# One VectorE instruction that scales, copies and reduces attention scores, and spare products for TensorE, in a fused attention and mixture-of-experts kernel

## The chip, the cores and the metric

The kernel runs on one core of a Trainium2 chip. A core has five engines, each with an in-order queue of its own: TensorE (PE in the profile; its weight loads are shown apart as PEld), VectorE (DVE), ScalarE (ACT), GpSimd (POOL) and SyncE (SP), whose queue issues nearly all DMAs of this kernel. The time of a run is the device time of one launch in microseconds (us); lower is better.

## The reference, cut to what matters

Two stages follow each other. The first is attention over 8 batches of 8 heads, 576 tokens of 64 numbers each, in which scores that lie more than `tau` below the row's maximum are dropped:

```python
scores = scale * np.matmul(q, k.transpose(0, 1, 3, 2))        # scale = 1/8
thresh = np.max(scores, axis=-1, keepdims=True) - tau
scores = np.where(scores >= thresh, scores, -1000000000.0)
scores = scores - np.max(scores, axis=-1, keepdims=True)
attn = np.exp(scores)
attn = attn / (np.sum(attn, axis=-1, keepdims=True) + 1e-09)
out = np.matmul(attn, v)
```

The second takes the 4608 rows of 512 numbers that this gives. Rows whose product with `w_skip` is positive go to one of 8 experts (the largest of 8 logits), each a two-layer network of 512 to 1024 to 512 with a ReLU between; the result is weighted by the gate and added to the row. The other rows are copied.

## The kernel before, in words

**Pairs, chunks, units.** The attention works on 32 pairs (8 batches, 4 pairs of heads each). A pair's q and k lie in one SBUF tile (`raw`), one head on partitions 0 to 63 and the other on 64 to 127. Its 576 query rows are cut into four chunks of 128 rows, in which each head is a unit of its own (`u`), and a last chunk (`M`) with the remaining 64 rows of both heads as a single unit. So a pair has nine units of 128 rows by 576 scores, and the kernel 288.

**What is done with a unit.** TensorE writes its scores in two rounds (`score`, line 519; `score_m`, line 529, for the chunk M) into PSUM. VectorE finds the negated maximum of each row (`top`, line 542, into a column of the tile `mx`). ScalarE computes exp(score - maximum) from PSUM into SBUF (`expo`, line 556). A small instruction (`thr`, line 549, VectorE or GpSimd) turns the maximum into the threshold. VectorE reads the scores from PSUM once more, compares them with the threshold and multiplies the exponential by the outcome (`mask`, line 564). The product is split into two half-precision parts, a rounded copy (`fph`, lines 329 and 331, ScalarE or VectorE) and the rest (`fpl`, line 618, mostly GpSimd). Two DMAs transpose the parts (line 623), and TensorE multiplies them with v (`av`, line 659, 30 products a chunk). The scale of 1/8 is put on q beforehand (`qs`, lines 357 and 359, once per pair).

**What a unit holds.** The eight banks of PSUM are shared out as six for scores (`sall`, three slots of two banks; a chunk takes two slots, the chunk M one), one for `gps` (transposes and logits) and one for the output of `av`. A score slot is given back by `mask`: `ring.free("sps", [k])` stands behind it. The exponentials have three buffers (`e`), the masked chunks two (`p`) and one (`pm`).

**What sets the order.** Every operation is put into a planner (`Plan`) with its engine or engines, a cost, the operations and buffers it depends on, and a key. `Plan.run` plays the program through with these costs: of the operations that are ready on an engine, the one with the smallest key comes next, and the order in which it starts them is the order in each engine's queue. The keys are the position in the sequence (nine per pair) plus an offset per kind of operation from the table `OFF`; a smaller one goes first. On the chip the queues keep this order and wait on semaphores. The planner also interleaves the preparation of v (`plan_v`), the logits of the experts and the bookkeeping of the routing.

**The second stage** begins when the attention's rows are in memory; its order is written out by hand behind `pl.run`, and the change leaves it alone.

Of the kernel before, what the change touches and what calls it, by code (L numbers as in the profile page):

```python
# [49 lines left out]
NBK = (NM + 1) * H + H // 2  # L50
NTL = NM * H
SPB = 3
GPB = 1
EB = 3
PFB = 2
HLB = 3
PTB = 3
TMB = 2
# [10 lines left out]
DISS = 0.65  # L69
DLAT = 0.9  # L70
OFF = dict(
    ld=-5.6, qs=49.8, S=-7.6, mx=-31.6, th=-71.4, e=-43.7, p=-83.3, ph=-25.7, pl=-26.3, tt=-8.5, av=4.9, cp=45.3, x=19.3, xw=3.1, row=126.2, rsp=-41.2, init=13.4, L1=-66.1, sc=-73.8, d0=50.9, phD=-64.0, v=8.8, vsp=4.8, V2=15.9,
)

class Op:
# [16 lines left out]

class Plan:
    def __init__(self):
        self.ops, self.rings = [], {}

    def take(self, name, bufs):
        return [(name, bufs)]
# [30 lines left out]
    def run(self, look):  # L129
# [14 lines left out]
        while left:  # L144
            best = None
            for e, c in cand.items():
                if not c:
                    continue
                if e == "PE":
                    c = [(max(free[e], x[0]) + (MODE[x[2].half] if x[2].half != half else 0.0), x[1], x[2]) for x in c]  # L150
                m = max(free[e], min(x[0] for x in c))
                x = min((x for x in c if x[0] <= m + look), key=lambda x: (x[1], x[0]))
                t = max(free[e], x[0])
                if best is None or t < best[0]:
                    best = (t, e, x[2])
            t, e, o = best
            o.t0, o.on = t, e
            if e == "PE":
                half = o.half
            o.t1 = free[e] = t + o.eng[e]  # L160
            for i, x in enumerate(o.xfer):
                link = max(link, t + (i + 1) * o.eng[e] / len(o.xfer) + DISS) + x
                o.t1 = link
            code = o.fn.__code__
            if code.co_argcount and code.co_varnames[0] == "e":
                o.fn(e)
            else:
# [12 lines left out]
def attn_moe_kernel(ctx: ExitStack, tc: tile.TileContext, qk, vl, vt, tau, wg, w1, w2, out):  # L180
# [17 lines left out]
    tpos = cp.tile([P, 1], F32, name="tpos")  # L198
    nc.vector.tensor_scalar(tpos, taub, 0.0, 0.125, op0=ALU.is_ge, op1=ALU.mult)
    wgt = cp.tile([P, NDT, 16], F32, name="wgt")  # L200
    onesr = cp.tile([1, P], F32, name="onesr")

    why = "a count of routed tokens bounds it"
    cnt = cp.tile([P, E], F32, name="cnt")
# [142 lines left out]
    def plan_pair(g):  # L347
        k = STEP * g

        def load():  # L350
            T["raw", g] = wtile(F32, "raw")[:, 0 : 2 * S]
            nc.sync.dma_start(T["raw", g], qk[g])

        def qs(e):
            q = T["raw", g][:, 0:S]
            if e == ACT:
                nc.scalar.activation(q, q, AF.Copy, scale=tpos)
            else:
                (nc.gpsimd if e == POOL else nc.vector).tensor_scalar(q, q, tpos, None, op0=ALU.mult)
# [133 lines left out]
    def plan_chunk(g, i):  # L493
# [44 lines left out]
        def top(u):  # L538
            if i == 0 and u == 0:
                T["mx", g] = ap_.tile([P, 2, STEP], F32, name="mx", tag="mx", bufs=3)  # L540
            c = 2 * i + u
            nc.vector.tensor_reduce(  # L542
                T["mx", g][:, 0, c : c + 1], bank(u), AX.XY, ALU.max, negate=True
            )

        def thr(e):
            cs = slice(2 * i, 2 * i + len(units))
            m = T["mx", g]
            (nc.gpsimd if e == POOL else nc.vector).tensor_scalar(
                m[:, 1, cs], m[:, 0, cs], -1.0, taue, op0=ALU.mult, op1=ALU.subtract  # L550
            )

        def expo(u):
            T["e", g, i, u] = e = ap_.tile([P, 2, HS], F32, name="e", tag="e", bufs=EB)
            c = 2 * i + u
            nc.scalar.activation(e, bank(u), AF.Exp, bias=T["mx", g][:, 0, c : c + 1])  # L556

        def mask(u):
            if M:
                T["p", g, i] = ap_.tile([P, 1, S], F32, name="pm", tag="pm", bufs=1)  # L560
# [12 lines left out]
        if M:  # L573
            ss = [pl.op(n + OFF["S"], score_m, [T["in", g]] + ring.take("sps", 3), {PE: 0.97}, half=True)]
        else:
            ss = []
            for r in range(2):
                ss.append(
                    pl.op(n + OFF["S"] + 0.1 * r, lambda r=r: score(r), [T["in", g]] + ring.take("sps", 3), {PE: 0.485}, half=True)
                )  # L580
        T.setdefault(("Sop", g), []).extend(ss)
        ms, es, ks = [], [], []
        for u in units:
            deps = ring.take("mx", 3) if i == 0 and u == 0 else [(T["m0", g],)]
            m = pl.op(n + OFF["mx"] + 0.1 * u, lambda u=u: top(u), ss + deps, {DVE: 0.67})
            if i == 0 and u == 0:
                T["m0", g] = m
            ms.append(m)
            es.append(pl.op(n + OFF["e"] + 0.1 * u, lambda u=u: expo(u), [m] + ring.take("e", EB), {ACT: 0.64}))
        t = pl.op(n + OFF["th"], thr, ms, {DVE: 0.12, POOL: 0.2})  # L590
        for u in units:
            take = [(ks[0],)] if u else ring.take("pm", 1) if M else ring.take("p", PFB)
            k = pl.op(n + OFF["p"] + 0.1 * u, lambda u=u: mask(u), [t, es[u]] + take, {DVE: 0.67})
# [163 lines left out]
    def plan_x(k, key, deps, src, last=False):  # L757
# [17 lines left out]
        t = pl.op(k, tr, deps + (ring.take("sps", SPB) if last else ring.take("gps", GPB)), {PE: 0.434})  # L775
# [999 lines left out]
```

## Time and profile before

| | |
|---|---|
| median of 3 runs | 1357.37 us (1357.23 to 1360.33) |
| profiled execution | 1357.51 us, of which the span from first to last instruction is 1355.7 us |
| busy in the span | TensorE 902.6 us, VectorE 815.8, GpSimd 579.2, ScalarE 465.6 |
| attention stage (0 to 1045 us of the span) | VectorE 665.3 us busy, TensorE 631.7, GpSimd 452.6, ScalarE 358.1 |
| second stage (1045 us to the end) | TensorE 270.8 of 311 us busy |

Busy time is the union of an engine's instructions. Matmuls are pipelined, so that a busy TensorE is not one at its peak. "PEclk" is the clock granted to TensorE as a share of full speed (2.4 GHz); it has two levels, 1.2 and 2.4 GHz, so that 0.67 is a mean over time. Each row of a group of instructions gives line, engine, operation, output and inputs by the program's names, shapes and count, then busy time and mean duration, then the engine's idle time just before these instructions and what ended it.

### The profile page before, as it was taken

The numbers are of one execution on the slowest core, as the hardware profiler recorded it, in microseconds if no ns is written. First come the engines' busy times: TensorE is split into PE (matmuls) and PEld (weight loads), VectorE is DVE, ScalarE is ACT, GpSimd is POOL, SyncE is SP. The second block draws the span as 40 slices with busy tenths as digits, with TensorE's granted clock in tenths as the row PEclk, the third lists the DMA queues.
The fourth block names the chain that finished last, engine by engine and source line by source line (L and its number), as shares of the span: only waits on it lengthen the run. The fifth ranks groups of instructions, "written<-read, shape, count | busy, mean of one in ns | idle before, by whom it ended". The sixth has DMA issues, their size and how long they took to land. (4 is left out here: it accounts for less than half of the span.)

```text
span 1355.7 us, 21156 instructions
## 1 busy us (share of the span) xinstructions
PE 902.6 (67%) x8210; PEld 696.9 (51%) x8210; DVE 815.8 (60%) x1422; ACT 465.6 (34%) x740; POOL 579.2 (43%) x394
## 2 busy tenths in 40 slices
PE   4555556656666565565565656766545688999996
PEld 3344334444445354344453544544425567989995
DVE  5667565676557667655666676557664234555872
ACT  2234322333334233323433333334233124435442
POOL 3443334343446435235553442446335205555552
PEclk7767766776667567577766665567667598999998
DMA  5655674676556765946584676565666226554540
GB/s 155 138 122 106 143 156 96 121 172 133 106 111 137 158 111 116 198 97 119 112 195 99 119 161 137 100 109 102 143 141 139 85 86 208 164 163 160 176 172 23
DMA packets 387781, 179.30 MB, mean 132 GB/s; under 512 B 354231, under 2 KB 354999, under 8 KB 387680
## 3 DMA queue, kind: packets, MB, share of 16 engines
q1 hardware_dynamic: 383056, 167.78, 56.0%
q0 software_dynamic: 4480, 10.15, 2.3%
q8 instruction: 65, 1.06, 0.3%
q14 instruction: 36, 0.29, 0.1%
q10 hardware_dynamic: 144, 0.00, 0.0%
HBM read 67.76 MB, written 24.65 MB: 68 GB/s over the span
## 5 line engine op out<-in xcount | busy, mean ns | idle before, releaser
L519 PE MATMUL sps<-raw 64*128 64x288 f32 x1024 | 267.7, 653 | 373.0 <-DVE p L564 306.0
L618 POOL TENSOR_TENSOR hla<-p,hla 128x1152 f16<-128x1152 f32 x119 | 282.5, 2374 | 392.4 <-ACT hla L329 206.4
L556 ACT ACTIVATE e<-sps,mx 128x576 f32<-128x576 f32 x288 | 199.7, 737 | 550.5 <-DVE mx L542 405.6
L519 PEld LDWEIGHTS sps<-raw 64*128 64x128 f32 x1024 | 129.9, 280 | 445.0 <-DVE p L564 230.7
L542 DVE TENSOR_REDUCE mx<-sps 128x1 f32<-128x576 f32 x288 | 206.1, 752 | 205.0 <-PE sps L519 103.8
L564 DVE SCALAR_TENSOR_TENSOR p<-sps,mx,e 128x576 f32<-128x576 f32 x256 | 197.7, 812 | 113.0 <-ACT e L556 102.8
L659 PEld LDWEIGHTS <-PTa 128*128 128x128 f16 x3840 | 181.8, 119 | 43.4 <-issue 35.9
L659 PE MATMUL avp<-Vh,PTa 128*128 128x65 f16 x2560 | 193.6, 225 | 3.3 <-DMA PTa<-hla 3.2
L659 PE MATMUL avp<-Vl,PTa 128*128 128x64 f16 x1280 | 184.1, 224 | 0.0
L1396 POOL TENSOR_TENSOR wl<-wr,wh 128x1024 fp32r<-128x1024 f32 x28 | 72.3, 2601 | 29.4 <-ACT wh L1395 24.1
L329 ACT ACTIVATE hla<-p 128x1152 f16<-128x1152 f32 x52 | 60.5, 1163 | 61.5 <-issue 49.4
L1433 PE MATMUL hps<-xh,wh 128*128 128x288 f32 (+4 forms) x224 | 69.1, 308 | 0.1
L1433 PE MATMUL hps<-xl,wh 128*128 128x288 f32 (+4 forms) x224 | 67.9, 303 | 0.0
L1433 PE MATMUL hps<-xh,wl 128*128 128x288 f32 (+4 forms) x224 | 67.8, 303 | 0.0
L709 POOL TENSOR_TENSOR xb<-a,z 128x512 f32<-128x512 f32 x32 | 39.0, 1218 | 55.3 <-DVE z L700 47.1
L1395 ACT ACTIVATE wh<-wr 128x1024 fp32r<-128x1024 f32 x60 | 60.6, 1050 | 0.0
L331 DVE CAST hla<-p 128x1152 f16<-128x1152 f32 x76 | 59.3, 780 | 1.0
L1495 PE MATMUL yps<-wh,QK 128*128 128x512 f32 (+2 forms) x224 | 57.5, 407 | 1.7 <-ACT wh L1395 1.5
L529 PE MATMUL sps<-raw 64*64 64x288 f32 (+2 forms) x320 | 58.1, 512 | 0.0
L1396 DVE TENSOR_TENSOR wl<-wr,wh 128x1024 fp32r<-128x1024 f32 x32 | 52.1, 1642 | 7.9 <-ACT wh L1395 7.4
L529 PEld LDWEIGHTS sps<-raw 64*64 64x64 f32 x320 | 33.1, 184 | 39.1 <-issue 29.7
L564 DVE SCALAR_TENSOR_TENSOR pm<-sps,mx,e 128x576 f32<-128x576 f32 x32 | 26.1, 817 | 43.2 <-PE sps L519 43.2
(241 smaller groups left out, 1429.6 us busy)
## 6 DMA issues: line engine op xcount, KB each, us to landing
wr<-in_w SPq DMA_DIRECT2D x31, 1024.0 KB
raw<-in_qk SPq DMA_DIRECT2D x32, 576.0 KB
vraw<-in_vl SPq DMA_DIRECT2D x32, 256.0 KB
out<-xb SPq DMA_DIRECT2D x32, 256.0 KB
xs<-xb SPq DMA_DIRECT2D x32, 256.0 KB
PTa<-hla SPq DMA_TRANSPOSE x256
vraw<-in_vt SPq DMA_DIRECT2D x8, 128.0 KB
TM<-hm SPq DMA_TRANSPOSE x64
```

What stands on the lines that cost most here:

```text
L329: nc.scalar.activation(dst, src, AF.Copy)
L331: nc.vector.tensor_copy(dst, src)
L519: nc.tensor.matmul(bank(h, j)[:, 0:HS], x[hs[h], i * P : i * P + P], x[hs[h], k0 : k0 + HS], start=True, stop=True)
L529: nc.tensor.matmul(bank(0, j)[hs[h], o : o + w], x[hs[h], NM * P : S], x[hs[h], S + c0 : S + c0 + w], start=True, stop=True, skip_group_ch ...
L542: nc.vector.tensor_reduce(T["mx", g][:, 0, c : c + 1], bank(u), AX.XY, ALU.max, negate=True)
L556: nc.scalar.activation(e, bank(u), AF.Exp, bias=T["mx", g][:, 0, c : c + 1])
L564: nc.vector.scalar_tensor_tensor(T["p", g, i][:, u].rearrange("p (a b) -> p a b", a=2), bank(u), T["mx", g][:, 1, c : c + 1], T.pop(("e", ...
L618: (nc.gpsimd if e == POOL else nc.vector).tensor_tensor(hl[:, lo0 : lo0 + w], T.pop(("p", g, i)).rearrange("p a b -> p (a b)"), hl[:, 0:w] ...
L659: nc.tensor.matmul(o[:, 0:e], x[:, w_, cs], y[:, vb, 0:e], start=first and j == 0, stop=kt == NM and j == 2, skip_group_check=True,)
L1395: nc.scalar.activation(w[0][:, sl], rs, AF.Copy)
L1396: lo[q % 2].tensor_tensor(w[1][:, sl], rs, w[0][:, sl].bitcast(F32), op=ALU.subtract)
L1433: nc.tensor.matmul(hp_[:, 0:cap], w_, x, start=(i == 0), stop=(i == len(mm) - 1))
```

## The change

`top` becomes one instruction that reads the scores from PSUM, multiplies them by -1/8, adds a tile of zeros (`none16`, bfloat16), writes the result to an SBUF tile `s` (four buffers) and writes its minimum to the column of `mx`. `expo` and `mask` read `s` in place of PSUM; `expo` writes into the chunk's tile `p`, and `mask` works on it in place, with `is_le` for `is_ge` since the sign is turned. The score slot is given back behind `top` (`ring.free("sps", [m])`). The scaling of q (`qs`) is gone, so that `score` depends on the load of `raw` alone. There are two score slots in place of three; of the two banks set free one goes to `gps` (two buffers) and one to `rest`, which nothing reads: where the plan leaves TensorE idle for more than 0.4 us, `fill` puts products of zeros (512 columns) into it, for six tenths of the rest of the gap at 0.22 us each. `p` has three buffers, `pm` two. The table `OFF` is replaced as a whole, and so the order of every queue of the attention stage.

```diff
-SPB = 3
-GPB = 1
-EB = 3
-PFB = 2
+GPB = 2
+SB = 4
+PFB = 3
+NSL = 2
+FILL = (0.4, 0.22, 0.6)
 OFF = dict(
-    ld=-5.6, qs=49.8, S=-7.6, mx=-31.6, th=-71.4, e=-43.7, p=-83.3, ph=-25.7, pl=-26.3, tt=-8.5, av=4.9, ...
+    ld=-63.5, qs=-113.0, S=-99.4, mx=-53.9, th=-2.3, e=-9.8, p=-0.5, ph=-18.0, pl=11.4, tt=-64.0, av=31.6, ...
 )
             if e == "PE":
+                if self.fill and free[e] > 0:
+                    gap = t - free[e] - FILL[0]
+                    for _ in range(int(gap * FILL[2] / FILL[1]) if gap > 0 else 0):
+                        self.fill(half)
                 half = o.half
...
-    sall = ps_s.tile([P, 6, 512], F32, name="sps")
-    slots = [(0, 1), (2, 3), (4, 5)]
+    sall = ps_s.tile([P, 2 * NSL, 512], F32, name="sps")
+    slots = [(2 * i, 2 * i + 1) for i in range(NSL)]
+    rest = ps_s.tile([P, 512], F32, name="rest")
...
-        qe = {POOL: 1.25, DVE: 0.42, ACT: 0.57} if g else {DVE: 0.42}
-        T["in", g] = pl.op(k - OFF["qs"], qs, [o], qe, off={DVE: OFF["d0"], ACT: OFF["d0"]} if g else {})
+        T["in", g] = o
...
-            nc.vector.tensor_reduce(
-                T["mx", g][:, 0, c : c + 1], bank(u), AX.XY, ALU.max, negate=True
+            T["s", g, i, u] = ap_.tile([P, S], F32, name="s", tag="s", bufs=SB)
+            nc.vector.tensor_tensor_reduce(
+                T["s", g, i, u].rearrange("p (a b) -> p a b", a=2),
+                bank(u),
+                none16[:, 0:S].rearrange("p (a b) -> p a b", a=2),
+                tneg8,
+                TOP,
+                ALU.add,
+                ALU.min,
+                T["mx", g][:, 0, c : c + 1],
             )
...
-            nc.scalar.activation(e, bank(u), AF.Exp, bias=T["mx", g][:, 0, c : c + 1])
+            nc.scalar.activation(
+                T["p", g, i][:, u], T["s", g, i, u], AF.Exp, bias=T["mx", g][:, 0, c : c + 1], scale=-1.0
+            )
...
             nc.vector.scalar_tensor_tensor(
-                T["p", g, i][:, u].rearrange("p (a b) -> p a b", a=2),
-                bank(u),
-                T["mx", g][:, 1, c : c + 1],
-                T.pop(("e", g, i, u)),
-                op0=ALU.is_ge,
-                op1=ALU.mult,
+                p, T.pop(("s", g, i, u)), T["mx", g][:, 1, c : c + 1], p, op0=ALU.is_le, op1=ALU.mult
             )
...
-            m = pl.op(n + OFF["mx"] + 0.1 * u, lambda u=u: top(u), ss + deps, {DVE: 0.67})
+            m = pl.op(n + OFF["mx"] + 0.1 * u, lambda u=u: top(u), ss + deps + ring.take("s", SB), {DVE: 0.67})
+            ring.free("sps", [m])
...
-            ring.free("sps", [k])
-            ring.free("e", [k])
+            ring.free("s", [k])
...
+    def fill(half):
+        r = D if half else P
+        nc.tensor.matmul(rest, none16[0:r, 0:P], none16[0:r, 0:512], start=True, stop=True, skip_group_check=True)
+    pl.fill = fill
```

## Rows read from the trace of the kernel before

**Rows 1.** Busy time of each engine in two stretches of the span, the attention stage and the rest: stretch, its length, then PE, PEld, DVE, ACT and POOL busy with the count of instructions, granted clock, mean busy share of the DMA engines, GB/s.

```profile
0.00:1045.00 1045.00, 631.74 (x6597) 454.80 (x6598) 665.29 (x1169) 358.08 (x558) 452.59 (x314) 0.67 0.64 129
1045.00:1356.00 311.00, 270.83 (x1618) 242.13 (x1616) 150.54 (x253) 107.51 (x182) 126.56 (x80) 0.92 0.42 141
```

**Rows 2.** Groups of instructions by line in the attention stage, shapes kept apart: busy us, mean ns of one, then the engine's idle us before them and what ended it.

```profile
L618 POOL TENSOR_TENSOR hla<-p,hla 128x1152 f16<-128x1152 f32 x119 | 282.5, 2374 | 392.4 <-ACT hla L329 206.4 <-issue 119.5 <-DVE hla L331 61.9
L542 DVE TENSOR_REDUCE mx<-sps 128x1 f32<-128x576 f32 x288 | 206.1, 752 | 205.0 <-PE sps L519 103.8 <-PE sps L529 72.6 <-ACT e L556 28.6
L556 ACT ACTIVATE e<-sps,mx 128x576 f32<-128x576 f32 x288 | 199.7, 737 | 550.5 <-DVE mx L542 405.6 <-DVE z L700 44.5 <-PE avp L659 35.8
L564 DVE SCALAR_TENSOR_TENSOR p<-sps,mx,e 128x576 f32<-128x576 f32 x256 | 197.7, 812 | 113.0 <-ACT e L556 102.8 <-POOL xb L709 5.8 <-issue 3.1
L564 DVE SCALAR_TENSOR_TENSOR pm<-sps,mx,e 128x576 f32<-128x576 f32 x32 | 26.1, 817 | 43.2 <-PE sps L519 43.2
```

**Rows 3.** Waits over the whole span: who waited for whom, us in total, times, longest us.

```profile
ACT e L556 <- DVE mx L542: 405.6, 120, 8.2
PE sps L519 <- DVE p L564: 306.0, 99, 6.3
...
DVE mx L542 <- PE sps L519: 103.8, 85, 2.8
DVE p L564 <- ACT e L556: 102.8, 111, 1.3
...
DVE mx L542 <- PE sps L529: 72.6, 32, 3.6
...
DVE pm L564 <- PE sps L519: 43.2, 29, 1.6
...
DVE mx L542 <- ACT e L556: 28.6, 32, 1.2
```

**Rows 4.** Instructions of all engines in order of time, from 502 to 519 us, neighbours of one kind merged: start us, us, engine, line, operation, tiles, count, and in brackets the engine's idle time before and who ended it.

```profile
502.07 1.24 PE L519 MATMUL sps<-raw 64*128 64x288 f32 x8 [1.04 <-DVE p L564]
...
503.24 1.69 PEld L659 LDWEIGHTS <-PTa 128*128 128x128 f16 x30
...
503.36 1.42 DVE L542 TENSOR_REDUCE mx<-sps 128x1 f32<-128x576 f32 x2 [0.55 <-PE sps L519]
...
504.90 1.37 ACT L556 ACTIVATE e<-sps,mx 128x576 f32<-128x576 f32 x2 [4.51 <-DVE mx L542]
...
506.36 1.54 DVE L564 SCALAR_TENSOR_TENSOR p<-sps,mx,e 128x576 f32<-128x576 f32 x2 [1.02 <-ACT e L556]
...
507.95 0.76 PE L519 MATMUL sps<-raw 64*128 64x288 f32 x4 [1.07 <-DVE vki L430]
...
509.76 1.88 PEld L659 LDWEIGHTS <-PTa 128*128 128x128 f16 x60
...
511.43 0.74 ACT L556 ACTIVATE e<-sps,mx 128x576 f32<-128x576 f32 x1 [3.84 <-DVE mx L542]
...
512.20 0.76 DVE L542 TENSOR_REDUCE mx<-sps 128x1 f32<-128x576 f32 x1 [0.89 <-ACT e L556]
...
518.38 2.29 PE L519 MATMUL sps<-raw 64*128 64x288 f32 x8 [0.91 <-DVE pm L564]
```

**Rows 5.** Single lines with the shortest, the median and the longest duration in ns: the masks of before, VectorE's subtraction of two SBUF tiles in two widths (the rows of line 618), a reduction of two numbers, and a ScalarE instruction of the same width that reads SBUF.

```profile
L564 DVE SCALAR_TENSOR_TENSOR p<-sps,mx,e x256: 799/816/820, 17.4 to 1033.3; 128x576 f32<-128x576 f32 x128
...
L618 DVE TENSOR_TENSOR hm<-pm,hm x13: 747/750/950, 47.6 to 811.3; 128x576 f16<-128x576 f32 x13
L618 DVE TENSOR_TENSOR hla<-p,hla x9: 1345/1351/1359, 114.0 to 1037.2; 128x1152 f16<-128x1152 f32 x9
...
L413 DVE TENSOR_REDUCE vmx<-vmx x8: 137/144/146, 15.8 to 822.1; 128x1 f32<-128x2 f32 x8
...
L357 ACT ACTIVATE raw<-raw,tpos x25: 758/772/783, 43.7 to 911.7; 128x576 f32<-128x576 f32 x25
```

**Rows 6.** The same view for VectorE instructions that read SBUF alone, and their groups' busy time and mean.

```profile
L549 DVE TENSOR_SCALAR mx<-mx,taue x138: 199/220/2400, 16.0 to 1031.2; 128x2 f32<-128x2 f32 x111, 128x1 f32<-128x1 f32 x27
...
L331 DVE CAST hm<-pm x25: 445/454/2020, 43.0 to 1003.2; 128x576 f16<-128x576 f32 x25
...
L549 DVE TENSOR_SCALAR mx<-mx,taue 128x2 f32<-128x2 f32 (+1 forms) x138 | 44.3, 339 | 0.6
L331 DVE CAST hm<-pm 128x576 f16<-128x576 f32 x25 | 24.9, 995 | 0.2
...
L1396 DVE TENSOR_TENSOR wl<-wr,wh x32: 1204/1224/7616, 1099.8 to 1329.4; 128x1024 fp32r<-128x1024 f32 x32
```

**Rows 7.** VectorE and GpSimd in order of time near 536 us: start us, us, engine, line, operation.

```profile
535.89 2.40 DVE L549 TENSOR_SCALAR mx<-mx,taue 128x2 f32<-128x2 f32 x1
...
535.91 2.36 POOL L618 TENSOR_TENSOR hla<-p,hla 128x1152 f16<-128x1152 f32 x1
```

**Rows 8.** A product of 512 columns in the second stage, and a stretch of that stage (columns as in the first group); then the load of q and k in SyncE's queue.

```profile
L1495 PE MATMUL yps<-wh,QK 128*128 128x512 f32 (+2 forms) x224 | 57.5, 407 | 1.7 <-ACT wh L1395 1.5 <-DVE QK L1465 0.2
...
1150.00:1200.00 50.00, 50.00 (x263) 44.25 (x261) 27.27 (x43) 20.13 (x31) 27.47 (x14) 1.00 0.56 185
...
SPq L352 <- PE sps L529: 49.2, 15, 7.4
```

More of the change, by code (lines that the diff above doesn't have):

```diff
@@ L52 @@
 SPB = 3
-GPB = 1
-EB = 3
-PFB = 2
+GPB = 2
+SB = 4
+PFB = 3
+NSL = 2
+TOP = 3.0e38
+FILL = (0.4, 0.22, 0.6)
 HLB = 3
@@ L71 @@
 OFF = dict(
-    ld=-5.6, qs=49.8, S=-7.6, mx=-31.6, th=-71.4, e=-43.7, p=-83.3, ph=-25.7, pl=-26.3, tt=-8.5, av=4.9, cp=45.3, x=19.3, xw=3.1, row=126.2, rsp=-41.2, init=13.4, L1=-66.1, sc=-73.8, d0=50.9, phD=-64.0, v=8.8, vsp=4.8, V2=15.9,
+    ld=-63.5, qs=-113.0, S=-99.4, mx=-53.9, th=-2.3, e=-9.8, p=-0.5, ph=-18.0, pl=11.4, tt=-64.0, av=31.6, cp=-20.0, x=28.2, xw=39.6, row=38.9, rsp=74.8, init=19.6, L1=-102.6, sc=-126.0, d0=16.6, phD=43.5, v=45.4, vsp=-12.1, V2=35.8,
 )
@@ L94, in __init__ @@
     def __init__(self):
-        self.ops, self.rings = [], {}
+        self.ops, self.rings, self.fill = [], {}, None
     def take(self, name, bufs):
@@ L197, in attn_moe_kernel @@
     nc.scalar.dma_start(taub, tau.rearrange("(a b) -> a b", b=1).broadcast_to([P, 1]))
-    tpos = cp.tile([P, 1], F32, name="tpos")
-    nc.vector.tensor_scalar(tpos, taub, 0.0, 0.125, op0=ALU.is_ge, op1=ALU.mult)
+    tneg8 = cp.tile([P, 1], F32, name="tneg8")
+    nc.vector.tensor_scalar(tneg8, taub, 0.0, -0.125, op0=ALU.is_ge, op1=ALU.mult)
     wgt = cp.tile([P, NDT, 16], F32, name="wgt")
     onesr = cp.tile([1, P], F32, name="onesr")
+    none16 = cp.tile([P, S], BF16, name="none16")
+    nc.vector.memset(none16, 0.0)
     why = "a count of routed tokens bounds it"
@@ L352, in load @@
             nc.sync.dma_start(T["raw", g], qk[g])
[L354 to L359, printed above, removed]
         o = pl.dma(k - OFF["ld"], load, ring.take("wr", WRB) + T["start"], [2.2], 0.46)
-        qe = {POOL: 1.25, DVE: 0.42, ACT: 0.57} if g else {DVE: 0.42}
-        T["in", g] = pl.op(k - OFF["qs"], qs, [o], qe, off={DVE: OFF["d0"], ACT: OFF["d0"]} if g else {})
+        T["in", g] = o
         if g == 0:
@@ L548, in thr @@
             m = T["mx", g]
-            (nc.gpsimd if e == POOL else nc.vector).tensor_scalar(
-                m[:, 1, cs], m[:, 0, cs], -1.0, taue, op0=ALU.mult, op1=ALU.subtract
-            )
+            (nc.gpsimd if e == POOL else nc.vector).tensor_scalar(m[:, 1, cs], m[:, 0, cs], taue, None, op0=ALU.add)
         def expo(u):
-            T["e", g, i, u] = e = ap_.tile([P, 2, HS], F32, name="e", tag="e", bufs=EB)
-            c = 2 * i + u
-            nc.scalar.activation(e, bank(u), AF.Exp, bias=T["mx", g][:, 0, c : c + 1])
-        def mask(u):
             if M:
-                T["p", g, i] = ap_.tile([P, 1, S], F32, name="pm", tag="pm", bufs=1)
+                T["p", g, i] = ap_.tile([P, 1, S], F32, name="pm", tag="pm", bufs=2)
             elif u == 0:
@@ L563, in mask @@
             c = 2 * i + u
-            nc.vector.scalar_tensor_tensor(
-                T["p", g, i][:, u].rearrange("p (a b) -> p a b", a=2),
-                bank(u),
-                T["mx", g][:, 1, c : c + 1],
-                T.pop(("e", g, i, u)),
-                op0=ALU.is_ge,
-                op1=ALU.mult,
+            nc.scalar.activation(
+                T["p", g, i][:, u], T["s", g, i, u], AF.Exp, bias=T["mx", g][:, 0, c : c + 1], scale=-1.0
+            )
+        def mask(u):
+            c = 2 * i + u
+            p = T["p", g, i][:, u]
+            nc.vector.scalar_tensor_tensor(
+                p, T.pop(("s", g, i, u)), T["mx", g][:, 1, c : c + 1], p, op0=ALU.is_le, op1=ALU.mult
             )
         if M:
-            ss = [pl.op(n + OFF["S"], score_m, [T["in", g]] + ring.take("sps", 3), {PE: 0.97}, half=True)]
+            ss = [pl.op(n + OFF["S"], score_m, [T["in", g]] + ring.take("sps", NSL), {PE: 0.97}, half=True)]
         else:
@@ L578, in plan_chunk @@
                 ss.append(
-                    pl.op(n + OFF["S"] + 0.1 * r, lambda r=r: score(r), [T["in", g]] + ring.take("sps", 3), {PE: 0.485}, half=True)
+                    pl.op(n + OFF["S"] + 0.1 * r, lambda r=r: score(r), [T["in", g]] + ring.take("sps", NSL), {PE: 0.485}, half=True)
                 )
@@ L588, in plan_chunk @@
             ms.append(m)
-            es.append(pl.op(n + OFF["e"] + 0.1 * u, lambda u=u: expo(u), [m] + ring.take("e", EB), {ACT: 0.64}))
+            take = [(es[0],)] if u else ring.take("pm", 2) if M else ring.take("p", PFB)
+            es.append(pl.op(n + OFF["e"] + 0.1 * u, lambda u=u: expo(u), [m] + take, {ACT: 0.64}))
         t = pl.op(n + OFF["th"], thr, ms, {DVE: 0.12, POOL: 0.2})
         for u in units:
-            take = [(ks[0],)] if u else ring.take("pm", 1) if M else ring.take("p", PFB)
-            k = pl.op(n + OFF["p"] + 0.1 * u, lambda u=u: mask(u), [t, es[u]] + take, {DVE: 0.67})
-            ring.free("sps", [k])
-            ring.free("e", [k])
+            k = pl.op(n + OFF["p"] + 0.1 * u, lambda u=u: mask(u), [t, es[u]], {DVE: 0.67})
+            ring.free("s", [k])
             ks.append(k)
@@ L773, in ev @@
             copy(e, xf, T.pop(("X", key)))
-        t = pl.op(k, tr, deps + (ring.take("sps", SPB) if last else ring.take("gps", GPB)), {PE: 0.434})
+        t = pl.op(k, tr, deps + (ring.take("sps", NSL) if last else ring.take("gps", GPB)), {PE: 0.434})
         x = pl.op(k + 0.3, ev, [t] + ring.take("xf", 2), {ACT: 0.478})
```

## The prediction, made before the changed kernel was run

> **What bounds the kernel now.** I begin with the busy times by stretch [rows 1]. In the second stage TensorE is busy for 271 of 311 us, and the change leaves that stage alone. In the attention stage no engine is full: VectorE, the busiest, has 665 of 1045 us and stands idle for 380; the granted clock of TensorE averages 0.67, between its levels of 1.2 and 2.4 GHz. So waits set the pace there. The groups by line tell where VectorE's idle time lies [rows 2]: 205.0 us before the reductions, 113.0 and 43.2 before the masks, 18.5 elsewhere. The list of waits names the partners [rows 3]: the reductions wait for scores (103.8 and 72.6 us), the masks for exponentials (102.8) and, in the chunk M, for TensorE (43.2), and TensorE's scores wait for masks (306.0). That is a ring, and the timeline shows it going round without overlap [rows 4]: scores 502.07 to 503.31, two reductions to 504.78, two exponentials to 506.27, two masks to 507.90, the next scores at 507.95. Each step begins about 0.1 us after the one before: 5.9 us a turn, of which VectorE works for 3. The third slot doesn't help, since a chunk needs two and gets the second only from a mask.
>
> **The change part by part.** All sums are made against the profiled execution (1357.5 us), 0.1 us above the median of the runs, so I take them as one.
>
> *The slot.* It now comes free behind the first VectorE step instead of behind the masks. Scores of the next chunk can then be made while VectorE masks, and by the keys (mx -53.9, p -0.5) the reduction goes ahead of a mask when both are ready. The exponential of one chunk lies beside VectorE's other work. Four buffers `s` allow two chunks in flight.
>
> *The new reduction* has no row. Nearest is the mask of before, which also reads PSUM and an SBUF tile and writes 128x576: 816 ns [rows 5]. Lower end: the reduction itself, 752 ns [rows 2]. Upper end: the mask plus a small reduction of 144 ns for reading out the minimum [rows 5], 960 ns. I take 816: 288 x (816 - 752) = +18 us (0 to +60).
>
> *The mask* now reads two SBUF tiles. Nearest: the subtraction of two SBUF tiles in the same width, 750 ns [rows 5], against 812 to 817: 288 x 63 ns = -18 us. The upper end is the wait below.
>
> *A new wait.* VectorE's instructions on SBUF alone are sometimes held up by GpSimd. A threshold, median 220 ns, took 2.40 us beside a GpSimd subtraction of 2.36 us and ended with it [rows 7]. The means stand above the medians: threshold 339 against 220, the cast of `pm` 995 against 454 [rows 6]. The masks of before, with one input in PSUM, never exceed 820 ns [rows 5]. The mask becomes an instruction that can be held. The two masks of a chunk run back to back, so there are 160 groups; ends 0 (as the masks of before) and 0.54 us (as the cast). Between 0.12 and 0.54 I take 0.3: 160 x 0.3 = +48 us (0 to +86). Behind a held mask stand the next reduction and so the slot, and TensorE waits for that.
> [...]
>
> VectorE's busy time becomes 665 + 18 - 18 + 48 = 713 us.
>
> *VectorE's idle time.* 18.5 us elsewhere stays. The masks' waits (102.8 and 43.2) all but go, since the exponential lies a chunk ahead and M's mask reads no PSUM: I leave 20. The single wait of a reduction for an exponential, 0.9 us once a pair and 28.6 us in all [rows 3, 4], shows that the column tile `mx` is guarded as a whole: a reduction follows the exponentials sent before it. Two exponentials (1.37 us) now lie beside two masks (1.4 us), so I leave the 28.6 as they are. The scores: 1.24 us a chunk at the high clock, 2.29 at the low one [rows 4], against about 2.1 us of other VectorE work (two masks, a threshold, at times a cast). At the high clock that covers them; at the low one, with 30 products of v in front (0.94 to 1.69 us [rows 4]) partly beside the reductions, about 0.5 us is missing. Today the scores cost 176.4 / 160 = 1.1 us a chunk; I take 0.6, which is 96 us (0 to 176). Sum: 18.5 + 20 + 28.6 + 96 = 163 us in place of 380.
>
> Attention 713 + 163 = 876 us against 1045: -169. Forecast 1357.5 - 169 = 1188, rounded to **1190 us**.
>
> *Edits at nothing.* Without `qs` ScalarE loses 25 instructions of 0.77 us [rows 5], beside its 687 us of idle time. The exponential reads SBUF: 0.77 in place of 0.74 us, on an engine that stays below half. More buffers of `p`, `pm` and `gps` can only take waits away. The loads of q and k (one DMA a pair) move behind the transposes, row stores and loads of v in SyncE's queue (key +63.5 in place of +5.6); four buffers and two pairs of lead hide that. If not, scores wait at each pair's start; the load's longest wait now is 7.4 us [rows 8], and 2 us a pair would be 64 us.
>
> *The fill.* A product of 512 columns took 57.5 / 224 = 0.26 us at clock 1.00 [rows 8]; at the lower clock I estimate twice that. TensorE idles for 413 us of the attention [rows 1]; if the plan's gaps were as long, six tenths at 0.22 us make at most 1,100 products, 290 us at the high clock. TensorE's 632 us at a mean of 0.67 are some 423 us at full clock, so 713 of 876 us would be taken: it fits, and a stage with TensorE at 50 of 50 us has clock 1.00 [rows 8]. At the low clock the products overrun their gaps (0.6 x 0.52 / 0.22 = 1.4 of each) and delay scores; I cost that between -60 us (clock up, scores always in time) and +60, and take 0, since the 0.6 us above stands for a mixed clock.
>
> **The rivals.**
> *1. GpSimd holds the masks (slower).* GpSimd's subtraction of 2.37 us starts behind the cast of its chunk, and at a shorter pace the next masks come just then; its share rises from 0.43 to above 0.5. For: rows 6 and 7. Against: the mean delays there are far below 2.37. From a mean wait of 0.3 + 169/160 = 1.35 us per mask group nothing is gained; at 1.5 us, 160 x 1.2 = 192 us more than forecast: 1380.
> *2. The mask takes two passes.* By the two widths of the subtraction [rows 5], 576 further elements cost 601 ns, so a mask would take 1351 ns: +173 us, of which longer cover for the scores gives back some 66 (96 to 30): attention 983, 1296. Against it: that subtraction runs at one pass with two SBUF inputs; but no row shows this instruction with two float SBUF inputs of size.
> The Trainium skill (Vector Engine (DVE) Microarchitecture Reference, Points that are easy to get wrong) says that this instruction's kind halves its throughput with two SBUF sources that aren't bfloat16. No row of before shows that form, so I give the case a chance of its own.
> *3. The order on the chip keeps exponentials and masks in series.* The guard on `mx`, and semaphores that release only after both units (the exponentials start 0.12 us after the second reduction [rows 4]), keep the masks' 102.8 us; the scores' waits fall to 60. Idle 18.5 + 102.8 + 10 + 28.6 + 60 = 220, attention 933: 1246.
> *4. All cover holds:* no held masks, 60 us idle, attention 726. But the DMA engines are busy for 0.64 x 1045 = 669 us [rows 1] and would have to run at 0.92; at 0.88 it is 760: 1073.
> *5. The DMAs hold the pace already,* and 0.64 is what the transposes allow: no change. Against: nothing in rows 3 waits for a transpose.
>
> **How the numbers follow.** Forecast 0.47 (own range 1110 to 1270), rival 1 0.12, rival 2 0.10, rival 3 0.18, rival 4 0.08, rival 5 0.05. Faster by over 0.3% (about what a measurement of this kernel can tell from no change): 0.83; within: 0.05; slower: 0.12. The range of 1070 to 1320 leaves out rivals 1 and 5 and little else; its ends take in the bounds of the reduction, of the waits and of the fill.
>
> **What would show it.** Attention near 876 us, VectorE over 0.8 busy in it; the wait of scores for masks gone and one for the new reduction in its place; reductions near 816 ns; masks with a minimum near 750 (rival 2: 1351) and a mean below 900 (rival 1: above 1400); clock above 0.75. I am wrong if masks still wait about 100 us for exponentials (rival 3), if TensorE runs full at a low clock, or if scores wait for `raw`.

## The result and the profile after

The changed kernel takes 1115.76 us (median of 3 runs, 1113.29 to 1115.98) against 1357.37 us: a ratio of 0.821, 95% interval 0.818 to 0.823. That is 241.6 us less; forecast were 167 us less.

The stretches of the profile after, cut where the attention ends (columns as in [rows 1]):

```profile
0.00:807.00 807.00, 594.50 (x6719) 410.83 (x6719) 733.46 (x1312) 413.77 (x596) 501.34 (x354) 0.79 0.79 164
807.00:1115.00 308.00, 279.90 (x1726) 248.44 (x1724) 159.11 (x276) 111.32 (x189) 135.69 (x87) 0.93 0.45 152
```

Nearly the whole gain lies in the attention: 807 us in place of 1045, while the second stage keeps its 308 (311). VectorE is busy for 733 of 807 us (0.91), before for 665 of 1045 (0.64). It is busy for 68 us longer and stands idle for 73.5 us in place of 379.7, which makes it the likely bound; the run with zeros below bears this out. The groups by line in the attention answer to [rows 2]:

```profile
L574 DVE SCALAR_TENSOR_TENSOR p<-s,mx,p 128x576 f32<-128x576 f32 x256 | 280.5, 1120 | 4.5 <-POOL mx L559 2.3 <-ACT p L567 1.6
L623 POOL TENSOR_TENSOR hla<-p,hla 128x1152 f16<-128x1152 f32 x102 | 263.5, 2586 | 56.9 <-ACT hla L339 27.1 <-issue 22.0 <-DVE p L574 2.6
...
L545 DVE CUSTOM_DVE_ANT_0 s<-sps,none,tneg 128x576 f32<-128x576 f32 x288 | 225.7, 810 | 54.6 <-PE sps L521 52.4 <-PE sps L531 1.7
...
L574 DVE SCALAR_TENSOR_TENSOR pm<-s,mx,pm 128x576 f32<-128x576 f32 x32 | 36.4, 1138 | 0.7 <-ACT pm L567 0.5 <-POOL mx L559 0.2
...
L545 DVE DVE_READ_ACCUMULATOR2_ANT mx<- 128x1 f32 x288 | 23.0, 80 | 0.0
```

VectorE's idle time before the reductions (the lines of `s`) fell from 205.0 to 54.6 us, before the masks of `p` from 113.0 to 4.5, before those of `pm` from 43.2 to 0.7. The mean of the masks of `p` rose from 812 to 1120 ns. The list of waits, against [rows 3]:

```profile
PE sps L521 <- DVE mx L545: 154.1, 85, 7.2
...
ACT p L567 <- DVE mx L545: 105.8, 51, 12.1
...
DVE s L545 <- PE sps L521: 52.4, 53, 2.8
```

TensorE's wait for masks (306.0 us) is gone; its wait is now for the reduction, and half as long. The masks' wait for exponentials (102.8) is down to the 1.6 us of the group above. What fills VectorE in their place shows in the order of time, beside [rows 4]:

```profile
412.35 2.37 POOL L623 TENSOR_TENSOR hla<-p,hla 128x1152 f16<-128x1152 f32 x1 [2.82 <-ACT hla L339]
412.46 0.08 DVE L545 DVE_READ_ACCUMULATOR2_ANT mx<- 128x1 f32 x1
412.46 0.81 DVE L545 CUSTOM_DVE_ANT_0 s<-sps,none,tneg 128x576 f32<-128x576 f32 x1
...
413.20 2.87 DVE L574 SCALAR_TENSOR_TENSOR p<-s,mx,p 128x576 f32<-128x576 f32 x2
...
413.33 2.29 PE L521 MATMUL sps<-raw 64*128 64x288 f32 x8 [7.23 <-DVE mx L545]
...
417.47 1.55 DVE L574 SCALAR_TENSOR_TENSOR p<-s,mx,p 128x576 f32<-128x576 f32 x2
417.60 1.62 PE L521 MATMUL sps<-raw 64*128 64x288 f32 x8 [0.22 <-DVE mx L545]
...
417.70 1.43 ACT L567 ACTIVATE p<-s,mx 128x576 f32<-128x576 f32 x2
418.40 2.85 POOL L623 TENSOR_TENSOR hla<-p,hla 128x1152 f16<-128x1152 f32 x1
```

Scores, masks and exponentials now begin within 0.25 us of each other (417.47 to 417.70), where they followed one another before. Two masks take 1.55 us when GpSimd is not subtracting as they start, and 2.87 when a subtraction of 2.37 us has begun before them (412.35). At 418.40 it is the other way about: the subtraction begins under a mask and takes 2.85. Counted over the trace, 61 of the 288 masks begin while GpSimd subtracts low parts, and their mean is 2012 ns; the 54 that meet no GpSimd instruction have a mean of 811 and none is over 820.

### The profile page after: what moved, and what is told of

The parts are those of the page before. It is cut to its first block, busy times and chain, and to the rows that moved or that the text cites. A ratio compares the mean times of both kernels' runs of the same rounds, so it can differ in the third digit from the quotient of the medians.

```text
span 1114.1 us, 21828 instructions
## 1 busy us (share of the span) xinstructions
PE 874.4 (78%) x8443; PEld 659.3 (59%) x8443; DVE 892.6 (80%) x1587; ACT 525.1 (47%) x785; POOL 637.0 (57%) x441
## 5 line engine op out<-in xcount | busy, mean ns | idle before, releaser
L521 PE MATMUL sps<-raw 64*128 64x288 f32 x1024 | 227.0, 558 | 155.8 <-DVE mx L545 154.1
L574 DVE SCALAR_TENSOR_TENSOR p<-s,mx,p 128x576 f32<-128x576 f32 x256 | 280.5, 1120 | 4.5 <-POOL mx L559 2.3
L545 DVE CUSTOM_DVE_ANT_0 s<-sps,none,tneg 128x576 f32<-128x576 f32 x288 | 225.7, 810 | 54.6 <-PE sps L521 52.4
L567 ACT ACTIVATE p<-s,mx 128x576 f32<-128x576 f32 x256 | 187.7, 768 | 152.6 <-DVE mx L545 105.8
L664 PEld LDWEIGHTS <-PTa 128*128 128x128 f16 x3840 | 157.4, 110 | 56.6 <-issue 51.1
L559 POOL TENSOR_SCALAR mx<-mx,taue 128x2 f32<-128x2 f32 (+1 forms) x88 | 71.9, 818 | 158.9 <-DVE mx L545 145.1
L339 ACT ACTIVATE hla<-p 128x1152 f16<-128x1152 f32 x113 | 130.1, 1155 | 49.3 <-DVE p L574 49.3
L1376 PE MATMUL rest<-none 64*128 64x512 bf16 (+1 forms) x233 | 86.0, 463 | 0.0
L531 PE MATMUL sps<-raw 64*64 64x288 f32 (+2 forms) x320 | 51.5, 463 | 36.8 <-DVE mx L545 36.3
L623 POOL TENSOR_TENSOR hm<-pm,hm 128x576 f16<-128x576 f32 x29 | 42.6, 1470 | 32.5 <-ACT hm L339 28.0
L339 ACT ACTIVATE a<-avp 128x260 f32<-128x260 f32 (+1 forms) x96 | 31.3, 344 | 63.4 <-PE avp L664 62.7
```

Source lines behind the costliest of these rows:

```text
L339: nc.scalar.activation(dst, src, AF.Copy)
L521: nc.tensor.matmul(bank(h, j)[:, 0:HS], x[hs[h], i * P : i * P + P], x[hs[h], k0 : k0 + HS], start=True, stop=True)
L531: nc.tensor.matmul(bank(0, j)[hs[h], o : o + w], x[hs[h], NM * P : S], x[hs[h], S + c0 : S + c0 + w], start=True, stop=True, skip_group_ch ...
L545: nc.vector.tensor_tensor_reduce(T["s", g, i, u].rearrange("p (a b) -> p a b", a=2), bank(u), none16[:, 0:S].rearrange("p (a b) -> p a b", ...
L559: (nc.gpsimd if e == POOL else nc.vector).tensor_scalar(m[:, 1, cs], m[:, 0, cs], taue, None, op0=ALU.add)
L567: nc.scalar.activation(T["p", g, i][:, u], T["s", g, i, u], AF.Exp, bias=T["mx", g][:, 0, c : c + 1], scale=-1.0)
```

## The experiments

The theory was that the slot's early release and the two engines working side by side give the gain, and that GpSimd's hold on the masks takes part of it back. The rivals were the new table of keys, the fill (through the clock), the new reduction by itself, and the buffers. Each measured ratio is against the kernel before; "stage" is the time to the end of the last mask, worked out from the trace (before 1034.8 us, of which VectorE 661.2 busy and 373.6 idle; after 796.8, 723.5 and 73.3). Where not all 288 masks are named, their mean is that of the 256 masks of `p`.

### The fill and the keys

```diff
-    pl.fill = fill
+    pl.fill = None
```

> The changed kernel without the spare products; the bank that they wrote stays unused. Theory A (the broken ring gives the gain: the slot comes free behind the first VectorE step, and VectorE, busy for 91% of the attention stage, is now the bound): granted clock of the attention stage falls from 0.79 to about 0.70, scores get slower and VectorE waits for them somewhat more, 1115 to 1150 us. Theory B (the clock gives the gain: 0.67 to 0.79): most of the 242 us is lost, 1250 us or more.

Measured: 1107.69 us, 0.816 (0.812 to 0.820), below theory A's range. The stretch of the attention, against the one above:

```profile
0.00:800.00 800.00, 539.89 (x6510) 390.20 (x6510) 734.63 (x1317) 414.39 (x597) 501.80 (x354) 0.78 0.79 166
```

The granted clock of the attention is 0.78 without the products and 0.79 with them, though TensorE is busy for 540 of 800 us without them and 594 of 807 with them. The fall to 0.70 that was expected did not come. So the fill neither raises the clock noticeably nor speeds the kernel; if anything it costs these 8 us, and the two intervals overlap.

The changed kernel with the old table of keys:

```diff
 OFF = dict(
-    ld=-63.5, qs=-113.0, S=-99.4, mx=-53.9, th=-2.3, e=-9.8, p=-0.5, ...
+    ld=-5.6, qs=49.8, S=-7.6, mx=-31.6, th=-71.4, e=-43.7, p=-83.3, ...
```

> The changed kernel with the key table of the kernel before (masks ahead of reductions again). Theory A (the ring was broken by the copy to SBUF, whatever the order): most of the gain stays, below 1220 us, with masks waiting for exponentials again in part. Theory C (the new order gives the gain): 1280 us or more.

Measured: 1153.55 us, 0.849 (0.845 to 0.854). VectorE is busy for 808 of the stage's 852 us; with the old keys it has more of the work, among it these thresholds, which GpSimd holds too:

```profile
L559 DVE TENSOR_SCALAR mx<-mx,taue 128x2 f32<-128x2 f32 x104 | 92.9, 894 | 1.1
```

The new keys are thus worth 38 us of the 242 (1153.6 to 1115.8), through what VectorE has to do rather than through its waits: its idle time is shorter here, 44 us. The same exchange in the kernel before, which gets the new table:

> The kernel before with the key table of the changed kernel, nothing else. Theory A (slots held until the mask keep the ring closed, whatever the order): 1320 to 1400 us, and the reductions' and masks' waits of about 350 us stay. Theory C (the keys brought the part of the gain that was left when the mask read PSUM again, 1226 us): 1200 to 1260.

Measured: 1389.86 us, 1.024 (1.020 to 1.027), slower by 32. The masks wait for exponentials for 119.1 us (102.8 before). The table alone gives nothing; of the kernels tried here it pays only in the one whose slot comes free early.

### Where the slot is given back, and where the exponential reads

In the next kernel the reduction copies to SBUF and the exponential reads the copy, but the mask reads PSUM and holds its slot, of which there are three again (`gps` has one bank, the fill is gone):

```diff
-            nc.vector.scalar_tensor_tensor(
-                p, T.pop(("s", g, i, u)), T["mx", g][:, 1, c : c + 1], p, op0=ALU.is_le, op1=ALU.mult
+            T.pop(("s", g, i, u))
+            nc.vector.scalar_tensor_tensor(
+                p.rearrange(...), bank(u), T["mx", g][:, 1, c : c + 1], p.rearrange(...), op0=ALU.is_ge, op1=ALU.mult
...
-            ring.free("sps", [m])
...
-            ring.free("s", [k])
+            ring.free("s", [es[u]])
+            ring.free("sps", [k])
```

> The changed kernel in which the mask alone reads the scores from PSUM again (threshold times -8, is_ge), so that a slot is held until the mask as before; PSUM is shared out as before (three slots, one bank for transposes, no bank and no products to spare). The SBUF copy and the exponential from it stay. Theory A: TensorE waits for masks again, 300 us or so, and the time returns to 1280 to 1400 us, though the masks are never held up (815 ns mean). Theories B and C, and any that puts the gain on the buffers or on the dropped scaling of q: below 1200 us.

Measured: 1226.06 us, 0.902 (0.897 to 0.907), between the ranges of the theories. TensorE waits for masks again:

```profile
PE sps L520 <- DVE p L574: 203.2, 97, 4.9
```

VectorE is idle for 214 us, and the masks have a mean of 811 ns. So over half of the gain remains although the slot is held to the mask. The same with the old keys:

> The mask reads PSUM again, three slots, no spare products, and the key table of the kernel before: what is left of the change is the SBUF copy with the exponential from it, the dropped scaling of q and a third buffer of p. Theory A': the copy lets the exponential leave the slot, but the slot is still held, 1230 to 1300 us, with VectorE waiting for scores as before and little for exponentials. Theory C (the keys): the masks wait for exponentials again by about 100 us and the time returns to 1320 to 1380.

Measured: 1233.03 us, 0.908 (0.904 to 0.913): it isn't the keys. What was left is the new reduction, the exponential's source, the buffers of `p` and the dropped scaling of q. First the kernel before, with the reduction alone exchanged (its copy is read by nobody):

```diff
-            nc.vector.tensor_reduce(
-                T["mx", g][:, 0, c : c + 1], bank(u), AX.XY, ALU.max, negate=True
+            sc = ap_.tile([P, S], F32, name="s", tag="s", bufs=4)
+            nc.vector.tensor_tensor_reduce(
+                sc..., bank(u), none16..., minus, 3.0e38, ALU.add, ALU.min, T["mx", g][:, 0, c : c + 1],
```

> The kernel before with only the reduction exchanged for the new instruction (scale -1, its copy of the scores is written and never read; exponential and mask read PSUM, q is scaled, the slots, buffers and keys are as before). In the trace of before a pair of reductions releases its readers once, after the second; in the changed kernel each new reduction releases by itself, after its readout. Theory E (that early release is what was left, 1226 to 1233 us, when the mask read PSUM again): the first exponential starts one reduction earlier in 128 chunks, 0.6 us each, so 1265 to 1300 us although each reduction is 0.15 us dearer. Theory F (reading the copy from SBUF, the third buffer of p or the dropped scaling of q did that): 1360 to 1400 us.

Measured: 1376.66 us, 1.014 (1.011 to 1.017). No gain came, and the instruction alone, with a copy that nobody reads, costs 19 us. But theory E itself was not tested by this run: in its trace the first reduction of a chunk releases nobody in any of the 128 two-unit chunks, just as before (160 releases for 288 reductions), and the first exponential begins 1.68 us after the first reduction. Then the kernel of 1233 us with one edit, the exponential from PSUM:

```diff
-                T["p", g, i][:, u], T["s", g, i, u], AF.Exp, bias=T["mx", g][:, 0, c : c + 1], scale=-1.0
+                T["p", g, i][:, u].rearrange("p (a b) -> p a b", a=2), bank(u), AF.Exp,
+                bias=T["mx", g][:, 0, c : c + 1], scale=0.125
```

> The run in which the mask read PSUM again with the old keys (1233 us), with one further edit: the exponential reads PSUM again too (scale 1/8). The copy is written and read by nobody; q stays unscaled, p keeps three buffers, the keys and the three slots are those of before. Theory G (an exponential that reads the SBUF copy waits for its own reduction alone, while one that reads PSUM also waits on TensorE and, merged with that, for both reductions of the chunk): the first exponential starts about 1.6 us after the first reduction begins, masks wait about 100 us for exponentials, and the time is 1340 to 1390. Theory H (the third buffer of p, the second of pm or the dropped scaling of q brought the 124 us): 1220 to 1260.

Measured: 1381.84 us, 1.018 (1.015 to 1.021). One operand of one instruction is 149 us, so the buffers of `p` and the dropped scaling, which this kernel keeps, are not what gave the gain. The order of time of both kernels, first with the copy:

```profile
492.24 0.82 DVE L544 CUSTOM_DVE_ANT_0 s<-sps,none,tneg 128x576 f32<-128x576 f32 x1 [0.69 <-PE sps L520]
...
492.98 0.81 DVE L544 CUSTOM_DVE_ANT_0 s<-sps,none,tneg 128x576 f32<-128x576 f32 x1
...
493.16 1.45 ACT L566 ACTIVATE p<-s,mx 128x576 f32<-128x576 f32 x2 [4.43 <-DVE mx L544]
...
494.72 1.54 DVE L574 SCALAR_TENSOR_TENSOR p<-sps,mx,p 128x576 f32<-128x576 f32 x2
```

and with the exponential from PSUM:

```profile
502.80 0.82 DVE L544 CUSTOM_DVE_ANT_0 s<-sps,none,tneg 128x576 f32<-128x576 f32 x1 [1.49 <-PE sps L520]
...
503.54 0.81 DVE L544 CUSTOM_DVE_ANT_0 s<-sps,none,tneg 128x576 f32<-128x576 f32 x1
504.28 0.08 DVE L544 DVE_READ_ACCUMULATOR2_ANT mx<- 128x1 f32 x1
...
504.48 1.37 ACT L566 ACTIVATE p<-sps,mx 128x576 f32<-128x576 f32 x2 [4.29 <-DVE mx L544]
...
505.88 1.54 DVE L575 SCALAR_TENSOR_TENSOR p<-sps,mx,p 128x576 f32<-128x576 f32 x2 [1.26 <-ACT p L566]
```

With the copy the first exponential begins 0.92 us after the first reduction began; from PSUM 1.68 us, behind the second reduction, and the masks then stand 1.26 us idle. Over the 128 two-unit chunks the last mask ends 4.12 us after the first reduction began in the one kernel, 5.19 in the other, 5.01 in the kernel before: 1.07 x 128 = 137 of the 149 us. The trace also tells why. With the copy all 288 reductions release a semaphore (a signal for which another engine's queue waits); from PSUM 165 do, and in the kernel before 160, one per chunk. The first reduction of a two-unit chunk releases in all 128 chunks with the copy, and in 5 from PSUM. An exponential that reads the banks waits there for its chunk as a whole and begins 0.12 us (median) behind the second reduction; one that reads the copy waits for its own reduction and begins 0.64 us before the end of the second. Masks wait for exponentials for 79.0 us (`p`) and 30.9 (`pm`) in the last kernel.

### The masks that GpSimd holds

GpSimd writes zeros in place of the subtraction, so it reads no SBUF there; the low parts of the probabilities are left out:

```diff
-            (nc.gpsimd if e == POOL else nc.vector).tensor_tensor(
-                hl[:, lo0 : lo0 + w], T.pop(("p", g, i)).rearrange("p a b -> p (a b)"), hl[:, 0:w], op=ALU.subtract
-            )
+            T.pop(("p", g, i))
+            (nc.gpsimd if e == POOL else nc.vector).memset(hl[:, lo0 : lo0 + w], 0.0)
```

> The changed kernel in which the subtraction that makes the low parts is replaced by writing zeros there, on the same engine and with the same planned cost: the low parts of the weights are left out. GpSimd then writes SBUF and reads none in this step. Theory A with masks held up by GpSimd's reads: the masks' mean falls from 1120 to about 830 ns, VectorE gets some 90 us shorter, and the time falls by 60 to 110 us, to 1005 to 1055. Theory D (the DMA engines, busy for 0.79 of the attention stage, are the bound now): the masks get shorter, but the time stays within 25 us of 1116. If the masks' mean stays above 1000 ns, it is not GpSimd's subtraction that holds them.

Measured: 980.73 us, 0.721 (0.717 to 0.725), 135 us below the changed kernel and below the range expected. The groups and the stretch of the attention:

```profile
L574 DVE SCALAR_TENSOR_TENSOR p<-s,mx,p 128x576 f32<-128x576 f32 x256 | 210.0, 844 | 8.0 <-ACT p L567 4.3 <-POOL mx L559 2.4 <-POOL xb L713 0.6
...
L624 POOL MEMSET hla<- 128x1152 f16 x102 | 108.3, 1068 | 40.1 <-DMA PTa<-hla 39.9
```

```profile
0.00:678.00 678.00, 532.99 (x6773) 375.62 (x6773) 589.98 (x1323) 412.00 (x598) 299.99 (x356) 0.89 1.00 195
```

The masks' mean falls from 1120 to 844 ns. VectorE's time, each moment counted once, falls by 141 us: masks 303.2 to 221.7, thresholds 38.9 to 14.8, its own share of the replaced step 36.8 to 14.6, the preparation of v 82.5 to 72.1. Of these, the third is work left out; in the others the same instructions run shorter, which I read as waiting for GpSimd inside them. That the writes hold no mask, and not only that they are shorter than the subtractions, shows in the masks that begin while GpSimd writes zeros: there are 40, with a mean of 848 ns, against 2012 for those that begin under a subtraction in the changed kernel. The DMA engines' share is now 1.00, and GpSimd waits 39.9 us for transposes, so that near 980 us the DMAs may well be the next bound.

The other way to keep a mask free is one input in PSUM. Here the exponential writes a PSUM tile of two banks, with one buffer (no fill, one bank for `gps`):

```diff
-                T["p", g, i][:, u], T["s", g, i, u], AF.Exp, ...
+                eps[:, :, 0:HS], T["s", g, i, u].rearrange("p (a b) -> p a b", a=2), AF.Exp, ...
...
-                p, T.pop(("s", g, i, u)), T["mx", g][:, 1, c : c + 1], p, op0=ALU.is_le, op1=ALU.mult
+                p, s2, T["mx", g][:, 1, c : c + 1], eps[:, :, 0:HS], op0=ALU.is_le, op1=ALU.mult
```

> The changed kernel with the exponential written to PSUM (one buffer of two banks, taken from the spare bank and one of the two for transposes; no spare products), so that the mask reads one tile of SBUF and one of PSUM, while the score slot still comes free behind the reduction. Nothing of the computation is left out. If the held masks are what VectorE loses: masks at 815 to 830 ns, VectorE some 90 us shorter in the attention stage, 1010 to 1060 us. If the single buffer puts each exponential behind the mask before it: masks wait for exponentials, 0.2 to 0.5 us a unit, 60 to 140 us, and the time stays at 1080 to 1150.

Measured: 1175.81 us, 0.866 (0.863 to 0.869), slower than either reading had it. The masks' shortest, median and longest duration, and the largest wait of ScalarE:

```profile
L575 DVE SCALAR_TENSOR_TENSOR p<-s,mx,eps x256: 750/808/815, 16.4 to 854.1; 128x576 f32<-128x576 f32 x128
```

```profile
ACT eps L563 <- DVE p L575: 221.3, 143, 4.3
```

No mask is held, but each exponential now waits for the mask before it to give back the single buffer. It confirms the hold's cause, but it is no way round it: all eight banks of PSUM are taken, so a second buffer could not be had.

Next, without the fill, GpSimd's subtraction in shorter pieces, two of 576 columns and four of 288 (the diff shows four):

```diff
+            n = 2 * len(units) if e == POOL else 1
+            for q in range(n):
+                a, b = q * w // n, (q + 1) * w // n
+                (nc.gpsimd if e == POOL else nc.vector).tensor_tensor(
+                    hl[:, lo0 + a : lo0 + b], pp[:, a:b], hl[:, a:b], op=ALU.subtract
+                )
```

> The changed kernel without the spare products, GpSimd's subtraction of 1152 numbers cut into two of 576 (1.27 us each by its rows of that width). If a mask waits for the whole GpSimd instruction that it meets, the wait is halved: masks' mean from 1114 to about 960 ns, VectorE some 45 us shorter, 1050 to 1085 us. If what counts is the sum of GpSimd's reads, whatever the pieces: masks above 1050 ns and 1100 us or more.

> The same with pieces of 288 (0.7 us each by estimate, half of 1.27 and a little). By the first reading: masks' mean about 900 ns, 1030 to 1075 us, unless GpSimd, which now waits for masks between its pieces, becomes late with the low parts (TensorE's products of v would then wait for transposes, over 20 us). By the second: no better than two pieces.

Measured: two pieces 1109.34 us, 0.817 (0.815 to 0.820), no change from the 1107.69 without the fill; the masks' mean is 1102 ns (1118). Four pieces give 1093.86 us, 0.805 (0.802 to 0.808), better than the second reading has it but short of the first, and the fastest kernel of this study that keeps the low parts:

```profile
L627 POOL TENSOR_TENSOR hla<-p,hla 128x288 f16<-128x288 f32 x408 | 370.9, 940 | 39.1 <-issue 19.7 <-ACT hla L339 16.7 <-POOL mx L559 1.3
L574 DVE SCALAR_TENSOR_TENSOR p<-s,mx,p 128x576 f32<-128x576 f32 x256 | 259.7, 1038 | 23.5 <-POOL mx L559 12.8 <-ACT p L567 10.1
```

The masks' mean falls to 1038 ns only. In place of 63 masks that begin under a subtraction, with a mean of 1933 ns, there are now 145 that begin under a piece, with a mean of 1185: more masks are held, each for less. That pieces wait for masks in turn is my reading of their mean of 940 ns against a median of 732. GpSimd's part takes 371 us in place of 264, and the next exponentials wait for it 99.7 us.

Last, without the fill, the threshold on ScalarE, to take 41 us from VectorE:

```diff
-            (nc.gpsimd if e == POOL else nc.vector).tensor_scalar(m[:, 1, cs], m[:, 0, cs], taue, None, op0=ALU.add)
+            nc.scalar.activation(m[:, 1, cs], m[:, 0, cs], AF.Identity, bias=taue)
```

> The changed kernel without the spare products and with the threshold on ScalarE (160 instructions of about 0.18 us) in place of VectorE or GpSimd. If VectorE is the bound: its 45 us of thresholds go and about as much of the time, 1060 to 1085 us. If the exponentials behind them on ScalarE come late, or VectorE is not the bound: 1100 us or more.

Measured: 1133.68 us, 0.835 (0.832 to 0.839), so the second reading came. The masks' mean rose to 1235 ns: 75 masks begin under a subtraction in place of 63, with a mean of 2189 ns in place of 1933. To the last mask, the masks give back 35 of the 41 us, and VectorE's other work, casts (10 us) and subtractions (9) among it, is 24 us longer in the plan's new order, so that it is busy for 742 us in place of 724.

## Why the prediction was right, and which term was mis-sized

The direction and the mechanism held: the ring of [rows 4] is open and VectorE is the likely bound. The median lies inside the range, 74 us under the forecast. In the stage, 876 us were forecast and 807 came; the sum was busy 713 and idle 163, measured 733 and 74. **The term that was mis-sized is the sum of VectorE's idle time**, 90 us too large:

- The scores were to cost 96 us; the reductions wait 54 for them, which I put down to the clock of 0.79 and to the held masks, which lengthen VectorE's cover between two reductions; no run takes the two apart.
- The 28.6 us of reductions waiting for exponentials were left in, by the guard on `mx`. They are gone: the reductions' 54.6 us of idle time are nearly all scores. They are gone already in the kernel of 1233 us, and back at 26.1 in the one of 1382, whose exponential reads PSUM: so it is the earlier exponential that removes them.
- The masks' wait for exponentials was left at 20, and is 2.

The busy time, each moment counted once and to the last mask (661.2 before, 723.5 after), by its terms:

- **The reduction**: forecast +18, measured +13 (205.3 to 218.1). Its duration is 810 ns, as the mask of before foretold (816). The readout of the minimum shows as an instruction of its own, 80 ns, but lies beside the next one (both begin at 412.46) and adds 2.4 us in all.
- **The mask**: -18 for its own duration and +48 for the hold, measured +80 together (223.2 to 303.2). The 18 us were not there; the hold is 0.50 us per group instead of 0.3, inside the bound of 0.54:

```profile
L574 DVE SCALAR_TENSOR_TENSOR p<-s,mx,p x256: 759/815/3781, 15.8 to 795.3; 128x576 f32<-128x576 f32 x128
```

- **Not forecast**: casts of masked chunks move to ScalarE (79.3 to 13.6 us on VectorE), while the subtractions on VectorE grow by 18 and the preparation of v by 31, a sum of -17; everything else -14. With the old keys the changed kernel has 35.0 us of casts and 41.4 of v (51.1 before), so the growth of v is the keys' and the fall of the casts only in part.

That the sum of the busy time came out near is partly luck: the masks took 50 us more than forecast, and terms that are not in the sum gave 31 of them back. The sign of a mean mask below 900 ns failed, at 1120.

The longest mask took 3781 ns, where the longest of before took 820 [rows 5]. The Trainium skill (SBUF — State Buffer, Who interferes with whom) says that two SBUF inputs on VectorE and a GpSimd read exclude each other, and that a GpSimd instruction which only writes doesn't count. Three runs here agree: mean 1120 ns beside subtractions, 844 beside zeros, and no mask over 815 ns with the exponential in PSUM. But the casts of `pm` in the kernel before read a single SBUF tile and were held all the same (mean 995 ns against a median of 454 [rows 6]): the long ones, 1.62 to 2.02 us, end 0.32 us behind a subtraction of GpSimd. One SBUF tile as the only input is no proof against the hold.

The rivals: **1** (GpSimd holds the masks) was true in kind and not in size, at 0.50 us per group against the 1.35 that would have used up the gain. **2** (two passes) fell: the median is 815 ns, not 1351. The rule of the Trainium skill (Vector Engine (DVE) Microarchitecture Reference, Points that are easy to get wrong) that this kind halves its throughput with two SBUF sources that aren't bfloat16 does not show in this kernel: the median is 815 ns with both in SBUF and 816 with one in PSUM. **3** fell by the 2 us. **4** (all cover holds, 1073) came nearest on the idle time, 60 assumed against 74, but had no held masks. **5** fell, though the DMA share of 1.00 in the run without low parts may show where it would begin. The **fill**, taken as 0, was right to 8 us, and the clock above 0.75 came without it (0.78).

What the prediction did not see is how the gain divides. Read as a path: 1357 to 1233 by the copy and the exponential that reads it, with the slot still held; to 1154 by masks from SBUF and the early slot, together with the new shares of PSUM (two slots for three) and the fill, which no run takes apart; to 1116 by the keys. It priced the exponential's new source at nothing, and named the joint release only under rival 3. The steps overlap, so that in another order each would have another share: once the slot comes free at the reduction, the exponential is off the path (masks wait 2 us for it). An exponential from PSUM beside an early slot was not tried, since the slot would have to wait for that read.

## What to carry to other kernels

Copying out of PSUM in the instruction that must read it anyway can pay twice: the bank comes free, and later readers wait for less. Before changing an operand's source, count how many releases its producer has in the trace; one per group instead of one per instruction can mean that its reader starts a whole group late, as here. And where the bound engine reads only SBUF beside a GpSimd that reads SBUF as well, compare each group's mean with its median: here the gap was time in which the other engine held it, and neither shorter pieces nor a moved threshold gave much of it back.

## What was not expected of the hardware

- The exponential's first start hangs on where it reads: 0.93 us after its chunk's first reduction began from SBUF (the kernel of 1233 us), 1.54 to 1.70 from PSUM (means over 128 chunks), with 288 against 160 to 165 releases. This is how the program was built, as its traces show it; what in the build decides it stays open.
- The accumulator's readout is an 80 ns instruction that costs almost nothing, 2.4 us for all 288, since the next instruction begins with it.
- A threshold on two numbers can be held as long as a large instruction: 894 ns on average with the old keys, against a median of 220 in the kernel before [rows 6].
- Products of zeros, 233 of them, left the granted clock of the stage where it was, 0.79 against 0.78.
